# Inner weight products in plain fp32, five pairs' sums on TensorE, the identity by DMA

## Chip, core and metric

The kernel runs on one core of one Trainium2 chip. The metric is device time in microseconds (us) of one execution; the time of a kernel is the median of its runs. The engines are TensorE (PE in the rows, its weight loads PEld), VectorE (DVE), ScalarE (ACT), GpSimd (POOL) and SyncE (SP), which issues the DMAs.

## What is computed

Attention with an exponential feature map over 8 batches, 8 heads, 576 positions, then two MLPs over the positions' 512 columns:

```python
# q, k, v: (8, 8, 576, 64), w_phi: (64, 128)
def phi(x):
    proj = x @ w_phi
    proj = proj - max(abs(proj), axis=-1)
    return concat([exp(proj), exp(-proj)], axis=-1)
kv  = sum_s phi(k)[s, f] * v[s, d]
z   = sum_s phi(k)[s, f]
x   = (phi(q) @ kv) / (phi(q) @ z + 1e-6)      # heads side by side: (8, 576, 512)

gate = sigmoid(causal_conv5(x, conv_w))        # per column
y    = (gate * (x @ w_val)) @ w_out            # first MLP

h   = relu(y @ w_in)                           # 512 -> 1024: u and v halves
v_n = normalize(v over its 512 columns)
out = (u * (w_spatial @ v_n + b_spatial)) @ w_out2
```

`w_val`, `conv_w`, `w_out`, `w_in` and the second `w_out` arrive as float64. `w_out` and `w_in` stand behind each other with nothing between, so the kernel forms their product once ("inner" weights `wg` for the half `v`, `wu` for the half `u`).

## The kernel before

The program is written as a plan: every instruction is added with the engines that could do it, the buffers it reads and writes and a key (its due time), and `Plan.order` sorts them into one queue for each engine with modelled durations, allocating two SBUF arenas on the way: `fa` (fp32, `FA_COLS` columns) and `ra` (fp32r, the rest of 28,880). Changing keys, an arena's size or an instruction therefore moves instructions on all engines. Copies out of PSUM may go to ScalarE or VectorE, as the plan decides. All ScalarE and VectorE work is recorded at one helper line (L378 before, L379 after), products at L434/L447 before and L435/L448 after, GpSimd at L413/L414, DMAs at L423/L424.

The work has three parts. *Weights* (`weights`): each float64 matrix is loaded as 128x1024 words, turned into fp32 by one ScalarE and four VectorE instructions (`load_f64`: ScalarE's absolute value, then two TENSOR_SCALAR and two SCALAR_TENSOR_TENSOR), and split by `split`/`parts` into a high and a low fp32r part (a copy, a subtraction on VectorE); a product of two such pairs takes three fp32r products (high x high, low x high, high x low). The inner weights are 4 blocks of 128x512 for `wg` and 4 for `wu`, each of 4 x 3 products (`gemm`); a block is copied to its high part by ScalarE and its low part by VectorE. *Attention* (`attention`), for 32 pairs of heads (4 per batch): load k and v (`load_k`), project k (`kproj`), exponentials (`kexp`), key-value sums (`kvacc`), feature sums z (`ksum` adds four blocks on VectorE, 2 + 2 instructions of 512 and 256 columns a head; `ztotal` sums over partitions on TensorE), a transpose against the identity (`kvturn`), project q (`qproj`), the maximum over partitions by GpSimd's `partition_all_reduce`, exponentials (`qexp`), `weigh` (es0 * z0 + es1 * z1: one ScalarE and one VectorE instruction of 576 columns a head), numerator and denominator on TensorE (`num`), and the division (`divide`), whose reciprocals go through DRAM (`rden`) to be broadcast. *MLP* (`mlp`) for each of the 8 batches, with `val` first: `wv` against x.

GpSimd's queue begins with `make_identity` (a memset and a select, masks.py), then memsets of `k4` and `v4`, the tiles that hold the last 64 positions of a pair's k and v in a block pattern, then of `ones`, `mine`, `s2`, `wr2`, and only then the maxima. SyncE's queue takes DMAs in the plan's order and waits in line for each buffer.

Of the kernel before, what the change touches and what calls it, by code (L numbers as in the profile page):

```python
# [34 lines left out]
AQ_LOAD, AQ_PROJ, AQ_EXP, AQ_NUM, AQ_HEAD, A_DIV = 0.1, 0.857, 1.733, 2.5, 0.965, 4.437  # L35
W_VAL, W_CONV, W_OUT, W_G, W_U, W_SP, W_OUT2, W_STEP = -1.593, -1.22, -0.852, -0.752, -0.564, -0.207, 0.466, 0.085
M_CONV, M_VAL, M_V, M_U, M_SP, M_OUT, M_ALL = -0.153, -0.295, -0.088, -0.004, 0.003, 0.195, 57.899
LONG_W, LONG_A, LONG_M = False, True, False
WINDOW = 0.341
FA_HOLD = 1000  # L40
RA_HOLD = 5009
PA_HOLD = 0
LATER = 0.161
# [289 lines left out]
def attn_moe_gmlp_kernel(  # L333
# [132 lines left out]
    ident_t = const.tile([128, 128], F32, name="ident")  # L466
    make_identity(nc, ident_t)
# [8 lines left out]
    convw = [fixed([128, 5], F32, f"convw{c}") for c in range(KD)]  # L476
# [9 lines left out]
    def load_f64(src, n):  # L486

        raw, w = fa.buf(2 * n), fa.buf(n)
        dma(raw.bitcast(U32), src.bitcast(U32))
# [17 lines left out]
    def weights():  # L507
# [14 lines left out]
        for hh in range(2):  # L522
            for r in range(2):
                fill(mine[hh][64 * r:64 * r + 64], float(r == hh))
        for x, value in ((s2, 1.0), (wr2, 0.0)):
            fill(x.f32()[64:128], value)
        for k in range(KD):
            at(W_VAL + W_STEP * k)
            split(load_f64(rows(w_val, k), DM), wv[0][k], wv[1][k])
# [36 lines left out]
        for k in range(KD):  # L566
            at(W_OUT2 + W_STEP * k)
            split(load_f64(rows(w_out2, k), DM), wo[0][k], wo[1][k])
# [67 lines left out]
    def ztotal(kva, sums, kpl):  # L636

        mms = []
        for first in (True, False):
            for j in range(4):  # L640
                hh, s = divmod(j, 2)
                o = kva[32 * j:32 * j + 32, 2 * F:3 * F]
                mms.append((o, ones, sums[:, F * j:F * j + F], True, False) if first
                           else (o, mine[hh], kpl[:, s], False, True))
        products(2 * 4 * F / 2400 + 0.1, mms, COLS4)

    def kvturn(kva):
# [4 lines left out]
        def run():  # L652
            for s in range(3):
                nc.tensor.transpose(real(tp)[:, F * s:F * s + F], real(kvT)[:, F * s:F * s + F], ident_t)  # L654

        plan.add({"PE": (0.35, 1.0, run)}, [kvT], [tp])
# [35 lines left out]
    def num(es, kv, ts):  # L692
# [9 lines left out]
        for j in range(2):  # L702
            copy(nd[:, js[j]], accs[j][:, 0:HALF])
        acc = psum()
        products(4 * HALF / 2400 + 0.05, [
            (acc[64 * hh + 32 * j:64 * hh + 32 * j + 32, 0:HALF], ones, ts[hh][:, js[j]], True, True)
            for j in range(2) for hh in range(2)
# [19 lines left out]
    def attention():  # L727
# [5 lines left out]
        for P in range(n):  # L733
# [10 lines left out]
            sums = fa.buf(4 * F)  # L744
            for hh in range(2):
                ksum(kp[hh], sums[:, 2 * F * hh:2 * F * hh + 2 * F])
            ztotal(kva, sums, kpl)
# [6 lines left out]
            for hh in range(2):  # L754
# [3 lines left out]
                ts.append(weigh(hh, es[hh], kv))  # L758
# [7 lines left out]
    def mlp(b):  # L766
# [5 lines left out]
        for c in range(KD):  # L772
# [6 lines left out]
                "ACT": act_way(a, x[:, 0:S], ACTF.Copy, scale=convw[c][:, 0:1]),  # L779
                "DVE": dve_way("tensor_scalar", out=a, in0=x[:, 0:S], scalar1=convw[c][:, 0:1], scalar2=None,  # L780
# [201 lines left out]
```

## Time and profile before

| | us |
|---|---|
| three runs | 909.77, 913.94 (median), 914.80 |
| profiled execution | 913.05 |
| its span | 911.3 |
| TensorE busy | 860.2 (94%) |
| VectorE busy | 724.6 (80%) |
| ScalarE busy | 533.6 (59%) |
| GpSimd busy | 154.7 (17%) |

The busy shares are means over a start of some 125 us, in which weights are prepared and the first pairs run, and a long part in which attention and MLP alternate. They are to be read by stretch, not over the whole span.

### The profile page before, as it was taken

Reading aid. Unit: us, or ns where it says so; the run is one execution under the profiler, and the core shown is the slowest. Engines: PE = TensorE matmul, PEld = TensorE weight load, DVE = VectorE, ACT = ScalarE, POOL = GpSimd, SP = SyncE. Lnnn points to the kernel's source line nnn. Section 1 sums busy time; section 2 is a strip of 40 time slices with the busy share of each in tenths; the row PEclk is TensorE's granted clock in tenths of the full one; section 3 lists DMA queues with packets and bytes.
Section 4 is the critical chain, followed back from the end, with each engine's and each line's share of the span. In section 5 each row is a group of like instructions: output and inputs, shape, how many; then the busy total and the mean of one; then the engine's idle time right before and its main releaser. Section 6 shows DMA issues by size and latency. Waiting matters only on the chain.

```text
span 911.3 us, 16890 instructions
## 1 busy us (share of the span) xinstructions
PE 860.2 (94%) x6224; PEld 679.8 (75%) x6224; DVE 724.6 (80%) x1674; ACT 533.6 (59%) x1124; POOL 154.7 (17%) x121
## 2 busy tenths in 40 slices
PE   4575999999999999999999999999999999999998
PEld 2342677688777888778777888778777888789896
DVE  3989999899869997589768997598768997497551
ACT  3577757675656765466557575475557665463231
POOL 3340121132012211113012211013011211100000
PEclk9787999999999999999999999999999999999999
DMA  7355313322221121221221121221220220101001
GB/s 219 102 151 155 104 54 89 100 84 61 68 78 44 43 77 50 65 60 50 80 62 37 53 86 47 72 60 51 79 64 31 70 64 31 32 21 37 24 6 58
DMA packets 60570, 61.94 MB, mean 68 GB/s; under 512 B 23366, under 2 KB 39878, under 8 KB 60488
## 3 DMA queue, kind: packets, MB, share of 16 engines
q1 hardware_dynamic: 60488, 60.87, 22.9%
q8 instruction: 49, 0.80, 0.4%
q14 instruction: 33, 0.27, 0.1%
HBM read 50.06 MB, written 9.58 MB: 65 GB/s over the span
## 4 chain that ended last, share of the span: by engine, by line
PE 77%; DVE 14%; DMA 3%; issue 3%; ACT 2%; POOL 1%; SPq 0%; ACTq 0%; DVEq 0%; POOLq 0%
PE bank L434 54%; PE bank L447 22%; DVE fa L378 12%; ACT fa L378 2%; DMA fa<-rden 1%; DVE ra L378 1%; DMA fa<-in_w_in_dram 1%; PE bank L654 1%; DMA fa<-in_w_out_dram 1%; POOL fa L413 0%; SPq L423 0%; DVE wu L378 0%; DVE wg L378 0%; ACT wv L378 0%; DVE ws L378 0%
## 5 line engine op out<-in xcount | busy, mean ns | idle before, releaser
L378 ACT ACTIVATE fa<-fa 128x576 f32<-128x576 f32 (+4 forms) x457 | 266.3, 624 | 115.7 <-DVE fa L378 92.2
L378 ACT ACTIVATE fa<-bank 128x288 f32<-128x288 f32 (+5 forms) x395 | 166.5, 451 | 165.6 <-PE bank L434 114.4
L413 POOL PARTITION_ALL_REDUCE fa<-fa x64 | 147.1, 2326 | 480.9 <-ACT fa L378 341.0
L378 DVE TENSOR_TENSOR fa<-fa 128x576 f32<-128x576 f32 (+4 forms) x368 | 171.3, 484 | 26.3 <-DMA fa<-rden 21.0
L447 PE MATMUL bank<-fa 128*64 128x288 f32 (+1 forms) x1024 | 136.1, 410 | 10.8 <-DVE fa L378 7.9
L378 ACT ACTIVATE ra<-fa 128x256 fp32r<-128x256 f32 (+5 forms) x211 | 94.8, 468 | 76.1 <-DVE fa L378 75.5
L378 DVE TENSOR_TENSOR ra<-fa,ra 128x256 fp32r<-128x256 f32 (+4 forms) x236 | 118.3, 522 | 10.4 <-ACT ra L378 10.0
L434 PE MATMUL bank<-wg,ra 128*128 128x512 f32 (+1 forms) x480 | 120.6, 401 | 0.0
L447 PEld LDWEIGHTS bank<-fa 128*64 128x64 f32 x1024 | 71.9, 140 | 63.1 <-issue 21.1
L434 PE MATMUL bank<-ws,ra 128*128 128x256 f32 (+1 forms) x768 | 113.7, 297 | 0.3 <-ACT fa L378 0.3
L434 PEld LDWEIGHTS bank<-ra,wu 128*128 128x128 f32 x768 | 104.0, 188 | 12.6 <-issue 7.7
L434 PE MATMUL bank<-ra,wu 128*128 128x256 f32 (+1 forms) x768 | 112.7, 298 | 0.0
L434 PEld LDWEIGHTS bank<-ws,ra 128*128 128x128 f32 x768 | 103.7, 188 | 9.4 <-issue 5.8
L434 PE MATMUL bank<-ra,wv 128*128 128x256 f32 (+1 forms) x768 | 109.1, 297 | 1.0 <-DVE fa L378 0.5
L378 DVE SCALAR_TENSOR_TENSOR fa<-fa 128x576 f32<-128x576 f32 (+4 forms) x208 | 103.7, 508 | 5.3 <-ACT fa L378 4.1
L434 PEld LDWEIGHTS bank<-ra,wv 128*128 128x128 f32 x768 | 102.6, 188 | 7.0 <-issue 2.8
L378 DVE SCALAR_TENSOR_TENSOR fa<-fa,convw 128x576 f32<-128x576 f32 x128 | 106.9, 856 | 1.1 <-ACT fa L378 0.9
L434 PE MATMUL bank<-wo,ra 128*128 128x512 f32 x432 | 106.1, 398 | 0.0
L434 PEld LDWEIGHTS bank<-wg,ra 128*128 128x128 f32 (+1 forms) x480 | 82.5, 177 | 29.6 <-issue 4.1
L434 PEld LDWEIGHTS bank<-wo,ra 128*128 128x128 f32 x432 | 79.4, 188 | 20.8 <-DVE fa L378 2.3
L378 DVE TENSOR_SCALAR fa<-fa 128x9 f32<-128x9 f32 (+9 forms) x199 | 56.6, 309 | 17.9 <-DMA fa<-fa 14.9
L378 DVE TENSOR_REDUCE fa<-bank 128x4 f32<-128x512 f32 (+1 forms) x96 | 51.4, 547 | 13.2 <-PE bank L447 13.0
(62 smaller groups left out, 650.0 us busy)
## 6 DMA issues: line engine op xcount, KB each, us to landing
fa<-in_qT_dram SPq DMA_DIRECT2D x32, 288.0 KB
fa<-rden SPq DMA_DIRECT2D x64, 144.0 KB
fa<-in_v_dram SPq DMA_DIRECT2D x32, 264.0 KB
fa<-in_kT_dram SPq DMA_DIRECT2D x32, 256.0 KB
out_dram<-fa SPq DMA_DIRECT2D x32, 256.0 KB
fa<-in_w_in_dram SPq DMA_DIRECT2D x8, 512.0 KB
fa<-in_w_val_dram SPq DMA_DIRECT2D x4, 512.0 KB
fa<-in_w_outT_dram SPq DMA_DIRECT2D x4, 512.0 KB
```

The lines of the kernel that those rows point to most:

```text
L378: return lambda: getattr(engine, method)(**{k: real(v) for k, v in kw.items()})
L413: getattr(nc.gpsimd, method)(*(real(a) for a in args), **{k: real(v) for k, v in kw.items()})
L434: nc.tensor.matmul(real(acc), lhsT=real(l), rhs=real(r), start=first and i == 0, stop=last and i == n - 1)
L447: nc.tensor.matmul(real(o), lhsT=real(l), rhs=real(r), start=first, stop=last)
L654: nc.tensor.transpose(real(tp)[:, F * s:F * s + F], real(kvT)[:, F * s:F * s + F], ident_t)
```

## The change

- The identity `ident` is no longer made by GpSimd: a zeroed tile is written to DRAM (`eye`), a column of ones to its diagonal, and `ident` is loaded from it, three DMAs on SyncE.
- GpSimd runs `partition_all_reduce` once on 4 columns of a zeroed tile `warm`, ahead of everything but the first memsets.
- The converted `w_out` and `w_in` are no longer split; the inner weights are formed by 4 plain fp32 products a block instead of 12 fp32r ones.
- For the first `EARLY` = 5 pairs the feature sums skip `ksum`: `ztotal` takes all four blocks of the exponentials (16 + 4 products instead of 4 + 4), and the denominator skips `weigh`: `num` takes z as weights against both exponentials (8 products instead of 4).
- The convolution weights are loaded into one tile, so that one conversion of 20 columns takes the place of four of 5.
- The plan's keys and holds, the arena's size and which arena end is used change, and with them the order everywhere.

```diff
-FA_COLS = 16416
+FA_COLS = 16944
 A_LEAD, A_RATE = 1.485, 1.0
-AK_LOAD, AK_SPLIT, AK_PROJ, AK_STEP, AK_ACC, AK_TURN = -1.619, -0.272, 0.647, -0.759, 0.582, 2.141
+AK_LOAD, AK_SPLIT, AK_PROJ, AK_STEP, AK_ACC, AK_TURN = -1.619, 0.008, 0.087, -0.449, 0.245, 2.141
...
-LONG_W, LONG_A, LONG_M = False, True, False
+LONG_W, LONG_A, LONG_M = True, False, True
...
-RA_HOLD = 5009
+RA_HOLD = 7101
...
+EARLY = 5
...
-    ident_t = const.tile([128, 128], F32, name="ident")
-    make_identity(nc, ident_t)
+    ident = fixed([128, 128], F32, "ident")
+    eye = Buf(dr.tile([128, 128], F32, name="eye"), 128)
+    warm = fixed([128, 8], F32, "warm")
...
+        fill(warm, 0.0)
+        pool(9.0, "partition_all_reduce", warm[:, 4:8], [warm], warm[:, 4:8], warm[:, 0:4], channels=128,
+             reduce_op=bass_isa.ReduceOp.absmax)
+        at(W_EYE)
+        zero, one = fa.buf(128), fa.buf(1)
+        fill(zero, 0.0)
+        dma(eye, zero)
+        fill(one, 1.0)
+        dma(eye.rearrange("a b -> (a b)")[0:128 * 128:129].unsqueeze(1), one)
+        dma(ident, eye)
...
-        for c in range(KD):
-            at(W_CONV)
-            copy(convw[c], load_f64(rows(conv_wT, c), 5))
+        at(W_CONV)
+        copy(convw, load_f64([rows(conv_wT, c) for c in range(KD)], 5 * KD))
         wot = []
         for c in range(KD):
             at(W_OUT + W_STEP * c)
-            wot.append(parts(load_f64(rows(w_outT, c), DM), DM))
+            wot.append(load_f64([rows(w_outT, c)], DM))
...
-                win.append(parts(load_f64(rows(w_in, c)[:, DM * e:DM * e + DM], DM), DM))
+                win.append(load_f64([rows(w_in, c)[:, DM * e:DM * e + DM]], DM))
...
-                gemm(acc, [
-                    t for (oh, ol), (ih, il) in zip(wot, win)
-                    for t in ((oh[:, ds], ih), (ol[:, ds], ih), (oh[:, ds], il))
-                ])
+                products(KD * 4 * DM / 2400, [
+                    (acc, o[:, ds], i, c == 0, c == KD - 1) for c, (o, i) in enumerate(zip(wot, win))
+                ], FULL)
...
+        mms, n = [], len(terms[0])
+        for i in range(n + 1):
             for j in range(4):
...
+                mms.append((o, ones, terms[j][i], i == 0, False) if i < n
+                           else (o, mine[j // 2], kpl[:, j % 2], False, True))
...
+        if ts:
+            terms = [[(ones, t)] for t in ts]
+        else:
+            z = [kv[:, 2 * F + 32 * i:2 * F + 32 * i + 32] for i in range(4)]
+            terms = [[(z[2 * hh + s], es[hh][s]) for s in range(2)] for hh in range(2)]
...
+            if P < EARLY:
+                terms = [[kp[j // 2][:, j % 2, F * c:F * c + F] for c in range(4)] for j in range(4)]
...
+                if P >= EARLY:
+                    ts.append(weigh(hh, es[hh], kv))
```

What moves where, word for word from the two orders (names: `k_`, `v_` are the k4 and v4 tiles, `fa`/`ra` the arenas, `bank` a PSUM bank; an ISA row without names is GpSimd's preparation for the call behind it).

GpSimd at the start, before:

```order
masks.py:197 MEMSET ident 128x128
masks.py:199 ISA
masks.py:199 AFFINE_SELECT ident<-ident 128x128
L413 MEMSET k_0_81 64x64 x2
...
L413 MEMSET mine_89 64x32 x2
L413 MEMSET s_90 64x512
L413 MEMSET wr_91 64x576
L413 ISA
L413 ISA fa<-fa 128x576 x4
```

and after:

```order
L414 MEMSET k_0_79 64x64 x2
...
L414 MEMSET mine_87 64x32 x2
L414 MEMSET warm 128x8
L414 ISA
L414 ISA warm<-warm 128x4
L414 MEMSET fa 128x128
L414 MEMSET fa 128x1
L414 MEMSET s_88 64x512
L414 MEMSET wr_89 64x576
L414 ISA fa<-fa 128x576 x4
```

The select ahead of the k4 memsets is gone, and the preparation for the maxima stands ahead of the dummy and the two fills for `eye` instead of ahead of the first real maximum.

VectorE up to the last instruction that the first wg products need, before (row 132, a subtraction of a split):

```order
L378 TENSOR_SCALAR fa<-fa 128x512
L378 SCALAR_TENSOR_TENSOR fa<-fa 128x512 x2
L378 TENSOR_TENSOR ra<-fa,ra 128x512
L378 SCALAR_TENSOR_TENSOR fa<-fa 128x512
...
L378 TENSOR_SCALAR fa<-fa 128x9
L378 SCALAR_TENSOR_TENSOR fa<-fa 128x576
L378 TENSOR_TENSOR ra<-fa,ra 128x512
```

and after (row 95, a conversion):

```order
L379 TENSOR_TENSOR fa<-fa 128x576
L379 TENSOR_SCALAR fa<-fa 128x512
L379 COPY fa<-bank_70 128x288
...
L379 SCALAR_TENSOR_TENSOR fa<-fa 128x512
L379 TENSOR_TENSOR fa<-bank_68,fa 128x512
L379 SCALAR_TENSOR_TENSOR fa<-fa 128x512
```

The subtractions into `ra` and the weighings (576 columns, SCALAR_TENSOR_TENSOR) are gone from the queue, and copies from PSUM have come in.

TensorE from the first wg block on, before:

```order
L447 MATMUL bank_67<-fa 64x288 x4
L447 MATMUL bank_71<-fa 64x288 x4
L434 MATMUL bank_72<-ra 128x512 x12
L434 MATMUL bank_74<-ra 128x512 x12
...
L434 MATMUL bank_73<-ra 128x512 x12
L447 MATMUL bank_74<-fa,ones 32x288 x4
L447 MATMUL bank_67<-wphi,k_2_83 128x128
```

and after:

```order
L448 MATMUL bank_69<-fa,wphi 128x288
L448 MATMUL bank_68<-fa 128x512 x4
L448 MATMUL bank_67<-fa 128x512 x4
...
L668 MATMUL bank_68<-ident,fa 128x128 x3
L448 MATMUL bank_69<-fa,v_1_83 128x256
L448 MATMUL bank_69<-fa 64x256 x8
L448 MATMUL bank_67<-fa 64x288 x4
L448 MATMUL bank_68<-fa 64x288 x4
L448 MATMUL bank_70<-fa 32x288 x8
L448 MATMUL bank_71<-wphi,k_2_81 128x128
```

A block has 4 products instead of 12, and a transpose and a pair's numerator (64x288) that stood ahead of the wg blocks now stand behind them; the first MLP product is row 129 in both orders.

## Rows read from the trace of the kernel before

**Rows 1.** Stretches: length, busy us of PE, PEld, DVE, ACT, POOL; clock; DMA share.

```profile
0.00:10.16 10.16, 0.00 (x0) 0.00 (x0) 0.00 (x0) 2.19 (x3) 0.95 (x8) 1.00 0.61 192
10.16:93.13 82.97, 52.45 (x367) 31.51 (x367) 74.06 (x146) 52.36 (x116) 26.36 (x30) 0.82 0.49 149
93.13:125.88 32.75, 30.44 (x170) 22.07 (x168) 32.18 (x56) 22.96 (x44) 2.17 (x1) 1.00 0.28 81
125.88:911.30 785.42, 777.34 (x5693) 626.20 (x5691) 618.36 (x1474) 456.07 (x963) 125.23 (x82) 1.00 0.20 57
13.02:94.62 81.60, 51.13 (x354) 30.49 (x355) 75.01 (x148) 53.44 (x119) 24.08 (x15) 0.81 0.47 143
```

**Rows 2.** The chain that ended last, in order: start us, us, what.

```profile
82.03 5.96 DMA fa<-in_w_in_dram
```

**Rows 3.** TensorE's timeline: start us, us, what xcount, idle before and its releaser.

```profile
10.16 0.80 PE L447 MATMUL bank<-wphi,k 128*128 128x128 f32 x2 [10.16 <-POOL k L413]
...
34.45 0.80 PE L447 MATMUL bank<-wphi,k 128*128 128x128 f32 x2
...
89.47 3.73 PE L447 MATMUL bank<-fa 128*64 128x288 f32 x16 [1.16 <-ACT fa L378]
...
93.13 5.81 PE L434 MATMUL bank<-ra 128*128 128x512 f32 x24
...
125.88 1.68 PE L434 MATMUL bank<-ra,wv 128*128 128x256 f32 x12
```

**Rows 4.** GpSimd's timeline, same columns.

```profile
9.52 0.28 POOL masks.py:199 TENSOR_SCALAR_AFFINE_SELECT ident<-ident 128x128 f32<-128x128 f32 x1 [8.58 <-issue]
...
19.71 5.03 POOL L413 PARTITION_ALL_REDUCE fa<-fa  x2 [5.99 <-DMA v<-in_v_dram]
```

**Rows 5.** DMA issues on SyncE's queue, same columns.

```profile
3.68 0.60 SPq L423 DMA_DIRECT2D k<-in_kT_dram  x1
...
15.01 0.43 SPq L423 DMA_DIRECT2D fa<-in_kT_dram  x1
...
52.68 0.47 SPq L423 DMA_DIRECT2D rden<-fa  x1
55.26 1.09 SPq L423 DMA_DIRECT2D fa<-rden  x2
```

**Rows 6.** ScalarE's timeline, same columns.

```profile
8.64 0.66 ACT L378 ACTIVATE fa<-fa 128x512 f32<-128x512 f32 x1 [6.63 <-DMA fa<-in_w_val_dram]
```

**Rows 7.** VectorE's timeline, same columns.

```profile
22.48 2.54 DVE L378 TENSOR_SCALAR fa<-fa 128x512 uint32<-128x512 uint32 x2
...
93.93 0.69 DVE L378 TENSOR_TENSOR ra<-fa,ra 128x512 fp32r<-128x512 f32 x1 [0.53 <-ACT ra L378]
```

**Rows 8.** VectorE's groups, 13 to 94.62: xcount | busy us, mean ns | idle before.

```profile
L378 DVE TENSOR_TENSOR ra<-fa,ra 128x512 fp32r<-128x512 f32 x9 | 7.5, 836 | 1.7 <-ACT ra L378 1.7
L378 DVE SCALAR_TENSOR_TENSOR fa<-fa 128x576 f32<-128x576 f32 x7 | 5.7, 814 | 0.9 <-ACT fa L378 0.9
L378 DVE TENSOR_TENSOR fa<-fa 128x512 f32<-128x512 f32 x8 | 5.5, 684 | 0.8 <-PE bank L447 0.8
L378 DVE TENSOR_TENSOR fa<-fa 128x256 f32<-128x256 f32 x8 | 3.3, 418 | 0.0
L378 DVE TENSOR_SCALAR fa<-fa 128x5 f32<-128x5 f32 x4 | 2.3, 620 | 0.0
```

**Rows 9.** TensorE's timeline, a pair's products in plain fp32.

```profile
51.88 2.16 PE L447 MATMUL bank<-fa 128*64 128x288 f32 x16
53.98 0.70 PE L447 MATMUL bank<-fa,v 128*128 128x256 f32 x2
54.61 1.95 PE L447 MATMUL bank<-fa 128*64 128x256 f32 x16
56.48 1.80 PE L447 MATMUL bank<-fa,wphi 64*128 64x288 f32 x8
...
105.77 0.69 PE L447 MATMUL bank<-fa,ones 128*32 128x288 f32 x8
```

More of the change, by code (lines that the diff above doesn't have):

```diff
@@ L9 @@
 from concourse._compat import with_exitstack
-from concourse.masks import make_identity
 F32 = mybir.dt.float32
@@ L475, in attn_moe_gmlp_kernel @@
     wr1 = fixed([128, S], F32R, "wr1")
-    convw = [fixed([128, 5], F32, f"convw{c}") for c in range(KD)]
+    convw = fixed([128, 5 * KD], F32, "convw")
     rden = [Buf(dr.tile([2, S], F32, name=f"rden{i}"), S) for i in range(4)]
@@ L488, in load_f64 @@
         raw, w = fa.buf(2 * n), fa.buf(n)
-        dma(raw.bitcast(U32), src.bitcast(U32))
+        m = 2 * n // len(src)
+        for i, x in enumerate(src):
+            dma(raw.bitcast(U32)[:, m * i:m * i + m], x.bitcast(U32))
         words = raw.bitcast(U32).rearrange("p (n t) -> p n t", t=2)
@@ L528, in weights @@
             at(W_VAL + W_STEP * k)
-            split(load_f64(rows(w_val, k), DM), wv[0][k], wv[1][k])
-        for c in range(KD):
-            at(W_CONV)
-            copy(convw[c], load_f64(rows(conv_wT, c), 5))
+            split(load_f64([rows(w_val, k)], DM), wv[0][k], wv[1][k])
+        at(W_CONV)
+        copy(convw, load_f64([rows(conv_wT, c) for c in range(KD)], 5 * KD))
         wot = []
@@ L567, in weights @@
             at(W_OUT2 + W_STEP * k)
-            split(load_f64(rows(w_out2, k), DM), wo[0][k], wo[1][k])
+            split(load_f64([rows(w_out2, k)], DM), wo[0][k], wo[1][k])
     xt = {}
@@ L634, in ksum, with ztotal @@
             op=ALU.add)
-    def ztotal(kva, sums, kpl):
-        mms = []
-        for first in (True, False):
+    def ztotal(kva, terms, kpl):
+        mms, n = [], len(terms[0])
+        for i in range(n + 1):
             for j in range(4):
-                hh, s = divmod(j, 2)
                 o = kva[32 * j:32 * j + 32, 2 * F:3 * F]
-                mms.append((o, ones, sums[:, F * j:F * j + F], True, False) if first
-                           else (o, mine[hh], kpl[:, s], False, True))
-        products(2 * 4 * F / 2400 + 0.1, mms, COLS4)
+                mms.append((o, ones, terms[j][i], i == 0, False) if i < n
+                           else (o, mine[j // 2], kpl[:, j % 2], False, True))
+        products((n + 1) * 4 * F / 2400 + 0.1, mms, COLS4)
     def kvturn(kva):
@@ L653, in run @@
             for s in range(3):
-                nc.tensor.transpose(real(tp)[:, F * s:F * s + F], real(kvT)[:, F * s:F * s + F], ident_t)
-        plan.add({"PE": (0.35, 1.0, run)}, [kvT], [tp])
+                nc.tensor.transpose(real(tp)[:, F * s:F * s + F], real(kvT)[:, F * s:F * s + F], real(ident))
+        plan.add({"PE": (0.35, 1.0, run)}, [kvT, ident], [tp])
         copy(kv, tp[:, 0:3 * F])
@@ L704, in num @@
         acc = psum()
-        products(4 * HALF / 2400 + 0.05, [
-            (acc[64 * hh + 32 * j:64 * hh + 32 * j + 32, 0:HALF], ones, ts[hh][:, js[j]], True, True)
-            for j in range(2) for hh in range(2)
+        if ts:
[3 more added lines that the diff above has]
+            terms = [[(z[2 * hh + s], es[hh][s]) for s in range(2)] for hh in range(2)]
+        n = len(terms[0])
+        products(n * 4 * HALF / 2400 + 0.05, [
+            (acc[64 * hh + 32 * j:64 * hh + 32 * j + 32, 0:HALF], w, x[:, js[j]], i == 0, i == n - 1)
+            for i in range(n) for j in range(2) for hh in range(2) for w, x in (terms[hh][i],)
         ], COLS4)
@@ L743, in attention @@
             at(t, AK_TURN)
[L744 to L747, printed above, removed]
+            if P < EARLY:
+                terms = [[kp[j // 2][:, j % 2, F * c:F * c + F] for c in range(4)] for j in range(4)]
+            else:
+                sums = fa.buf(4 * F)
+                for hh in range(2):
+                    ksum(kp[hh], sums[:, 2 * F * hh:2 * F * hh + 2 * F])
+                terms = [[sums[:, F * j:F * j + F]] for j in range(4)]
+            ztotal(kva, terms, kpl)
             kv = kvturn(kva)
@@ L757, in attention @@
                 at(t, AQ_HEAD * hh + AQ_NUM)
-                ts.append(weigh(hh, es[hh], kv))
+                if P >= EARLY:
+                    ts.append(weigh(hh, es[hh], kv))
             nd, dn = num(es, kv, ts)
```

16 lines of the change are left out of this document (8 added, 8 removed).

## Prediction

> **What bounds the kernel now.** I cut the span into stretches first, then read the start in detail. The stretches [rows 1] tell where TensorE's missing 51 us of 911.3 are: 10.16 before its first product, 82.97 − 52.45 = 30.5 between 10.16 and 93.13, 2.3 between 93.13 and 125.88, and only 8.1 in the 785.42 us from the first product of the MLP (125.88) to the end. Between 10.16 and 93.13 it also works at a mean granted clock of 0.82, from 93.13 on at 1.00. So from 93.13 on TensorE is the limit, and what the change can win lies before. There VectorE sets the pace: it can only begin at 13.02, when the first projection is out, and from then to 94.62 it works for 75.01 of 81.60 us [rows 1]. The chain agrees: it runs through VectorE's conversions and one weight load (82.03, 5.96 us [rows 2]) before TensorE takes over.
>
> Three landmarks on TensorE matter [rows 3]: the first product at 10.16, released by a memset of GpSimd; the first inner weight product (wg) at 93.13; the first MLP product (wv) at 125.88. The changed order has the same six key projections, six query projections, five key-value sums, four numerators and four denominators ahead of the last landmark, so the kernels can be compared landmark by landmark.
>
> **Start of the span.** GpSimd does nothing until 9.52 (8.58 us without a releaser), then the select; the memsets of k4 behind it release TensorE at 10.16 [rows 3, 4]. The change takes the select away, so the memsets run from 0.8 on, and the first product waits for its loads: the last one of k4 is issued at 3.68 [rows 5]. The row next to it is the first w_val load, 32 times as large, issued at 4.96 and used by ScalarE at 8.64: 3.7 us [rows 5, 6]. The shortest trip here is rden's, written from 52.68 and read from 55.26: 2.6 us [rows 5]. So the k4 data is there between 6.3 and 7.4; I take 6.7. That moves TensorE, and VectorE behind it, forward by 3.5 us (2.8 to 3.9): VectorE begins at 9.5 instead of 13.02.
>
> The pause of 5.99 us before the first real maximum [rows 4] now falls before the dummy, between about 3.5 and 12. I count no gain for that beyond the 3.5: the maximum waits for projections that come 3.5 earlier. Its price: the first maxima ran 2.5 us each, and two VectorE instructions under them took 2.54 us together [rows 4, 7]. The dummy has 4 columns instead of 576, and no row shows such a size: it holds VectorE up by between 0 and 2.5 us. I take 0, since most of it falls before VectorE has much to do, and keep 2.5 for the range. The Trainium skill, GPSIMD Engine Reference, section 8 (Key points), has a rule against this part: GpSimd shares its SBUF interfaces with VectorE, with contention for VectorE instructions in a 2-port mode or with two SBUF inputs. The 2.54 us row agrees; by the rule the sum would be worse by up to the same 2.5 us.
>
> The identity's three DMAs stand on SyncE's queue between the convolution weights and pair 2's loads. Each takes SyncE 0.3 to 0.7, two wait for the one before (2.6 us as for rden), the first for a buffer that VectorE gives back. So pair 2's loads, issued from 15.01 on [rows 5], go out up to 8 us later. Pair 2's projection ran at 34.45 [rows 3]: the cover is over 10 us, and I cost it at nothing; without cover it would be those 8 us.
>
> **VectorE's work before the inner products.** Up to 94.62 it takes 147 instructions, the last being the subtraction at 93.93 that the wg products need [rows 7]. The changed order needs 103, to the last conversion of w_outT. By groups [rows 8]: nine splits of inner weights 9 × 0.836 = 7.5 us; seven weighings for denominators 7 × 0.814 = 5.7; eight and eight feature sums 8 × 0.684 + 8 × 0.418 = 8.8; of the convolution weights' sixteen small instructions, four of which took 2.3, four are left, about 3.3 less; part of one w_in load that no longer comes ahead, 3.1. Together 28.4. Back come three copies from PSUM and part of one more key exponential, 3.2. Net 25 of 86.5.
>
> Wall time per summed time was 81.60/86.5 = 0.94. If that stays, the remaining 61 take 58 us. If instead what disturbs VectorE stays whole (the ten 576-column instructions, most of them behind maxima, are ten in both orders), only undisturbed time goes: the groups sum to 86.5 where VectorE was busy 75.01, so each of 147 begins 0.08 before the one ahead ends, a 128x512 one is worth 0.60, and the same count gives 18.8 net: 62.8 us. With the start at 9.5 the last conversion is done between 67.5 and 72.3. The first inner block needs it only for its last quarter, 2.7 us after it began, so the block starts between 64.8 and 72.3. I take **70**, near the slower end because of those maxima, against 93.13: 23.1 us earlier. ScalarE (53.44 of 81.60 us busy [rows 1], with nine copies fewer) doesn't bind. Six of the eight weight loads for wg stand on SyncE's queue ahead of pair 0's rden write, the last one right behind pair 1's, at about 61 by VectorE's order, so it has some 5 us in hand.
>
> **TensorE from the first inner product to the first MLP product.** Before: 32.75 us, 30.44 busy, 23.1 of it in 96 fp32r products of 128x512 (0.24 each: 5.81 for 24 [rows 3]). After: 32 plain fp32 products of this size, which the trace lacks. Bounds from fp32 rows, start to start [rows 9]: a 128x128x256 one takes 0.63 with a change of tiling behind it (53.98 to 54.61), and 256 further columns cost 1.87/4 = 0.47 (54.61 to 56.48), so at most 1.10. Without the change of tiling two pairs of column halves give 1.87/4 for 256 and 2.10/4 for 288 columns (51.88 to 53.98), both 1.82 ns a column, so 0.93. Less is not excluded, since these run two side by side and may hinder each other: an fp32r product of 512 columns loses nothing of the kind at 0.24, so I let it go down to 0.85. I take 0.93, because four such products run back to back on one bank: 29.8 us.
>
> Also in this stretch now: pair 3's numerator (2.1), a transpose (0.5), twelve more column products for a feature sum and four for a denominator. A denominator's four took 0.69 [rows 9], so 0.7 and 3 × 128/288 × 0.69 = 0.9. Sum: 30.4 − 23.1 + 29.8 + 4.2 = 41.3 busy and 2.3 idle as before, 43.6: 10.9 more than 32.75. VectorE's instructions there sum to about 34, so TensorE sets the end. The other four feature sums and three denominators lie before 70, where TensorE was idle for 30 of 83 us: 4 × 0.9 + 3 × 0.7 = 5.7 more, nothing on the path. After the first MLP product one denominator of the five is left: 0.7.
>
> **Sum.** 911.3 − 23.1 + 10.9 + 0.7 = 899.8 of span; the profiled execution took 913.05, 1.75 more than its span, so 901.5, and as the forecast **901**. That execution lies 0.9 below the median of the three runs (913.94; 909.77 to 914.80), so 0.5%, 4.6 us, is about what can be told from no change.
>
> **Rivals.**
> (a) VectorE's disturbances shrink in proportion and TensorE finds no idle time: inner products at 64.8, the stretch 2.3 shorter: 901.5 − 5.2 − 2.3 = 894. For it: VectorE idles little even now. Against: the maxima, nine before 94.62, stay about as many.
> (b) The weights come no earlier: their loads wait in line on SyncE behind rden and k4 loads, as in the chain's 5.96 us load. If the inner products start at 82 to 87, the longer fp32 stretch eats the rest: 913.5 to 918.5. Against: DMA works at half its share there (0.49 [rows 1]), and six of the loads now stand before pair 0's rden write, where three did.
> (c) Slower: TensorE runs the fp32 block at the lower of its two clock levels (1.2 GHz). A pair's numerator took 3.73 us at 89.47 after an idle gap, 2.16 at 51.88 [rows 3, 9]. All the way at that level the 32 products cost 29.8 us more: 931. It decides from the point where half of them run low (916). Against: the stretch from 93.13 on had 1.00 in the dense work of the block itself [rows 1].
> (d) The whole program's order is new, and the last 785 us are no longer kept at 99%: one per cent more idle is 7.9 us, so 909. VectorE works 618 of 785 us there [rows 1], which speaks against more.
>
> **How the numbers follow.** Forecast 0.55, (a) 0.13, (b) 0.13, (c) 0.06, (d) 0.13. The range, 892 to 912, reaches from (a) with 0.85 per product (2.6 less) over 907 (1.10 per product, 5.4 more) and (d), with the late start of 72.3 on top, to the edge of (b). Faster by over 0.5% takes the forecast, (a) and over half of (d): 0.76. Within 0.5%: the rest of (d) and most of (b), 0.15. Slower: (c) and the far end of (b), 0.09.
>
> **What would show it.** The first product near 6.7 and VectorE's first row near 9.5; the dummy before 14; wg products from about 70 at 0.93 us each and a granted clock of 1.00; the first wv product near 113.6; the rest within 2 us of 786. If the wg start lies above 80, the loads or a new wait on VectorE are to blame and the term of 23.1 is wrong; if 32 products take over 34 us, that of 29.8; if the rest is over 790, it was wrong to take the long part as unchanged.

## The result, and the profile after

The changed kernel took **902.6 us** (median of 4 runs, 900.6 to 904.75), the kernel before 912.69 in the same series (4 runs, 909.77 to 914.80): ratio 0.9892, 95% interval 0.9853 to 0.9931. The forecast was 901 with a range of 892 to 912. The profiled execution took 900.6, the lowest of the four; its span is 898.8.

The three landmarks of the prediction cut the span. The columns are those of [rows 1]: length, busy time of TensorE, its weight loads, VectorE, ScalarE and GpSimd, granted clock, DMA share, GB/s.

```profile
7.11:71.77 64.66, 49.75 (x467) 30.52 (x467) 54.66 (x103) 38.90 (x83) 20.63 (x15) 0.92 0.61 183
71.77:110.47 38.70, 38.32 (x188) 18.49 (x186) 32.95 (x58) 23.94 (x45) 4.55 (x3) 1.00 0.36 106
110.47:898.80 788.33, 776.98 (x5701) 630.69 (x5699) 633.50 (x1496) 445.67 (x933) 128.24 (x82) 1.00 0.21 57
```

TensorE's timeline at the same places, to be laid beside [rows 3] (a plain fp32 product of 128x512 stands as two records, so x8 is a block of four products):

```profile
7.11 0.77 PE L448 MATMUL bank<-wphi,k 128*128 128x128 f32 x2 [7.11 <-DMA k<-in_kT_dram]
...
71.77 3.70 PE L448 MATMUL bank<-fa 128*128 128x512 f32 x8
75.68 7.13 PE L448 MATMUL bank<-fa 128*128 128x512 f32 x16 [0.21 <-DVE fa L379]
82.99 3.70 PE L448 MATMUL bank<-fa 128*128 128x512 f32 x8 [0.17 <-DVE wg L379]
...
95.05 14.00 PE L448 MATMUL bank<-fa 128*128 128x512 f32 x32
...
110.47 6.01 PE L435 MATMUL bank<-ra,wv 128*128 128x256 f32 x48
...
123.92 2.15 PE L448 MATMUL bank<-fa 128*32 128x288 f32 x16 [3.19 <-ACT fa L379]
```

| landmark, us | before | forecast | after |
|---|---|---|---|
| first product | 10.16 | 6.7 | 7.11 |
| first inner product | 93.13 | 70 | 71.77 |
| from there to the first wv product | 32.75 | 43.6 | 38.70 |
| from there to the end | 785.42 | 786.1 | 788.33 |
| span | 911.3 | 899.8 | 898.8 |

The inner products begin 21.4 us earlier, their stretch is 6.0 longer, the rest 2.9 longer: 911.3 − 21.4 + 6.0 + 2.9 = 898.8. The chain that ended last runs through a weight load that is issued beside the first inner block and lands behind it (75.48), then through TensorE up to the first wv product, and behind that through a load of the spatial weights, which ends in the wait of 3.19 us above.

```profile
70.54 4.94 DMA fa<-in_w_in_dram
...
87.02 22.03 PE bank L448 x140
...
111.46 9.56 DMA fa<-in_w_spT_dram
```

### The profile page after: what moved, and what is told of

Same layout as the page of the kernel before. It is cut to its first block, busy times and chain, and to the rows that moved or that the text cites. A ratio compares the mean times of both kernels' runs of the same rounds, so it can differ in the third digit from the quotient of the medians.

```text
span 898.8 us, 17083 instructions
## 1 busy us (share of the span) xinstructions
PE 865.1 (96%) x6352; PEld 679.7 (76%) x6352; DVE 721.1 (80%) x1655; ACT 509.8 (57%) x1061; POOL 156.4 (17%) x123
## 4 chain that ended last, share of the span: by engine, by line
PE 81%; DVE 8%; DMA 5%; ACT 3%; issue 2%; SPq 1%; DVEq 0%; ACTq 0%
PE bank L435 53%; PE bank L448 27%; DVE fa L379 7%; ACT fa L379 2%; PE bank L668 1%; DMA fa<-in_w_spT_dram 1%; DMA fa<-in_w_in_dram 1%; DMA fa<-rden 1%; SPq L424 1%; DVE ra L379 1%; DMA fa<-fa 0%; DMA k<-in_kT_dram 0%; DMA rden<-fa 0%; DMA v<-in_v_dram 0%; DVE wg L379 0%
## 5 line engine op out<-in xcount | busy, mean ns | idle before, releaser
L379 ACT ACTIVATE fa<-fa 128x576 f32<-128x576 f32 (+2 forms) x447 | 257.1, 624 | 123.8 <-DVE fa L379 95.1
L379 ACT ACTIVATE fa<-bank 128x288 f32<-128x288 f32 (+4 forms) x352 | 149.9, 453 | 164.0 <-PE bank L435 86.5
L379 DVE TENSOR_TENSOR fa<-fa 128x2 f32<-128x2 f32 (+4 forms) x348 | 161.8, 481 | 53.6 <-DMA fa<-rden 37.4
L448 PE MATMUL bank<-fa 128*64 128x256 f32 (+3 forms) x1168 | 168.1, 420 | 10.3 <-ACT fa L379 9.8
L448 PEld LDWEIGHTS bank<-fa 128*64 128x64 f32 (+2 forms) x1168 | 84.8, 140 | 83.4 <-issue 32.0
L379 ACT ACTIVATE ra<-fa 128x256 fp32r<-128x256 f32 (+4 forms) x198 | 86.6, 461 | 80.8 <-DVE fa L379 67.8
L379 DVE TENSOR_TENSOR ra<-fa,ra 128x256 fp32r<-128x256 f32 (+4 forms) x224 | 104.2, 490 | 15.3 <-ACT ra L379 12.8
L379 DVE SCALAR_TENSOR_TENSOR fa<-fa 128x2 f32<-128x2 f32 (+4 forms) x192 | 95.1, 499 | 11.1 <-ACT fa L379 8.4
L379 DVE SCALAR_TENSOR_TENSOR fa<-fa,convw 128x576 f32<-128x576 f32 x128 | 103.8, 828 | 0.0
L379 DVE TENSOR_SCALAR fa<-fa 128x512 f32<-128x512 f32 (+8 forms) x190 | 56.5, 321 | 11.3 <-ACT fa L379 6.3
```

What stands on the lines that cost most here:

```text
L379: return lambda: getattr(engine, method)(**{k: real(v) for k, v in kw.items()})
L448: nc.tensor.matmul(real(o), lhsT=real(l), rhs=real(r), start=first, stop=last)
```

## Experiments

A table of start keys sets the order of the whole program here, so an edit can be undone in two ways: with the order made anew by the table of the changed kernel, or with its order held. The ratio is to the kernel before in the same series (911.93 us for e1 to e9, 912.26 for h1 to h4, 912.84 for the last four). The times are medians, the landmarks and spans those of one profiled execution each; that of t1 took 900.95 and that of t2 911.66, the lowest of theirs. Where the order is made anew, the work ahead of a landmark can differ too.

| run | us | ratio to before (95%) | first product | first inner | first wv | span |
|---|---|---|---|---|---|---|
| changed kernel | 902.6 | 0.9892 (0.9853–0.9931) | 7.11 | 71.77 | 110.47 | 898.8 |
| e9, larger ring only | 917.56 | 1.0060 (1.0042–1.0078) | 7.22 | 68.48 | 125.22 | 915.8 |
| e1, EARLY = 0 | 927.27 | 1.0171 (1.0154–1.0188) | 7.38 | 79.75 | 134.39 | 924.1 |
| e2, inner weights in fp32r | 911.9 | 0.9987 (0.9969–1.0005) | 7.49 | 70.91 | 116.60 | 907.7 |
| e3, start as before | 911.92 | 1.0001 (0.9983–1.0020) | 9.83 | 72.05 | 130.10 | 911.2 |
| h1, VectorE +1 | 917.39 | 1.0053 (1.0028–1.0077) | 7.38 | 82.15 | 124.89 | 915.7 |
| h2, VectorE +3 | 946.04 | 1.0376 (1.0350–1.0402) | 7.24 | 97.53 | 146.00 | 942.8 |
| h3, dummy first | 901.28 | 0.9887 (0.9863–0.9911) | 7.33 | 71.89 | 110.32 | 898.7 |
| h4, half the inner products | 900.64 | 0.9872 (0.9855–0.9889) | 7.22 | 71.40 | 111.13 | 899.0 |
| h6, half as many again | 914.52 | 1.0023 (1.0006–1.0041) | 7.47 | 70.24 | 121.76 | 912.8 |
| h7, late start | 906.65 | 0.9931 (0.9906–0.9955) | 11.49 | 74.83 | 113.39 | 905.2 |
| t1, fp32r, own table | 904.84 | 0.9911 (0.9884–0.9938) | 8.89 | 71.58 | 113.46 | 899.0 |
| t2, EARLY = 0, own table | 913.96 | 1.0012 (0.9995–1.0029) | 7.17 | 72.58 | 120.76 | 909.6 |

### The order by itself

```diff
-FA_COLS = 16944
+FA_COLS = 17200
```

> The changed kernel with nothing but a larger ring of buffers (17200 columns of FA_COLS instead of 16944). No work is added or taken away; the planner only orders it a little differently. It is the control for the next run, which needs this ring, and it prices what a re-planned order alone does. Both theories below: landmarks within 2 us of the changed kernel's (first product 7.1, first inner product 71.8, first wv product 110.5, span 898.8), time within 3 us of it. If it lies further off, an order that only happens to be better or worse is worth as much as the edits, and differences of that size between the other runs say little.

Measured: 917.56, 15.0 us over the changed kernel, with the same instructions in another order. Both theories expected 3 at most.

```profile
7.22:68.48 61.26, 45.16 (x393) 26.66 (x393) 53.10 (x99) 37.86 (x82) 20.55 (x15) 0.92 0.58 180
68.48:125.22 56.74, 50.68 (x278) 25.13 (x278) 35.24 (x60) 29.08 (x56) 7.41 (x5) 0.94 0.28 85
125.22:915.80 790.58, 776.53 (x5683) 631.14 (x5681) 633.17 (x1495) 441.96 (x925) 123.06 (x81) 1.00 0.20 57
```

The inner products even begin 3.3 us earlier, but TensorE's busy time from the first product to the first wv product is 95.84 instead of 88.07 us (16 records more, and a clock of 0.94 in the second stretch) and its idle time 22.2 instead of 15.3; the rest is 2.3 longer. So with an order that fits less well, the edits end no better than the kernel before, and a run that undoes one edit under this table shows the edit and the misfit together. The next three have to be read so.

```diff
-FA_COLS = 16944
+FA_COLS = 17200
...
-EARLY = 5
+EARLY = 0
```

> The changed kernel with EARLY = 0: the feature sums and weighings of the first five pairs are back on VectorE, and TensorE no longer makes them (ring of 17200 columns). Theory V (VectorE's instructions ahead of the inner products set when these begin): about 24 more of them stand before the last inner weight conversion, some 11 to 14 us of VectorE; the first inner product moves from 71.8 to 81 to 86, the stretch up to the first wv product gets 1.6 us shorter because TensorE has less to do there, and the time rises by 8 to 12 us, to about the time of the kernel before. Rival R (the weights' loads, or merely the new table of start keys, set the start): the first inner product stays within 3 us of 71.8, and the time within 3 us of 901.

Measured: 927.27, 24.7 over the changed kernel, but 9.7 over the control with its ring (e9), the first inner product at 79.75, 11.3 later than there.

```diff
-FA_COLS = 16944
+FA_COLS = 16416
...
-            wot.append(load_f64([rows(w_outT, c)], DM))
+            wot.append(parts(load_f64([rows(w_outT, c)], DM), DM))
...
-                products(KD * 4 * DM / 2400, [
-                    (acc, o[:, ds], i, c == 0, c == KD - 1) for c, (o, i) in enumerate(zip(wot, win))
-                ], FULL)
+                gemm(acc, [
+                    t for (oh, ol), (ih, il) in zip(wot, win)
+                    for t in ((oh[:, ds], ih), (ol[:, ds], ih), (oh[:, ds], il))
+                ])
```

> The changed kernel with the inner weights again split in two parts and multiplied as three fp32r products (96 instead of 32). Theory V: five to eight splits of 0.6 to 0.8 us return to VectorE ahead of the first inner product and the others behind it; it begins 4 to 7 us later, at 76 to 79; TensorE's block of inner products takes 23.1 instead of 27.9 us, so that the stretch to the first wv product falls from 38.7 to about 34, unless VectorE's splits then set it; the time is within 3 us of the changed kernel's: the plain fp32 products win on VectorE what they cost on TensorE. Rival R: the start stays at 71.8, the block is 4.8 us shorter, and the time falls by 5 us, to about 896.

Measured: 911.9. The first inner product is at 70.91, neither later by 4 to 7 us nor with a gain behind it. The ring is that of the kernel before, so the order is another as well. Against a misfit of up to 15 us this prices nothing.

```diff
+    make_identity(nc, ident_t)
...
-        pool(9.0, "partition_all_reduce", warm[:, 4:8], [warm], warm[:, 4:8], warm[:, 0:4], channels=128,
-             reduce_op=bass_isa.ReduceOp.absmax)
...
-        dma(ident, eye)
```

> The changed kernel with the identity built on GpSimd again and without the dummy maximum. Theory V: the first product is at 10.2 instead of 7.1, VectorE's first row at 13.0 instead of 9.9, and all behind it is later by 3.1 us: first inner product at 75, time +3 us, about 904.5. Rival R1 (the start is not passed on, since the loads set the inner products' start): the first inner product stays at 71.8, time unchanged. Rival R2 (the dummy and the three DMAs cost as much as the early start brings): first inner product at 71 to 72 in spite of the first product at 10.2.

Measured: 911.92, three times the loss expected, with the first inner product at 72.05 and the first wv product at 130.10. The order moved again: 68 records of TensorE more stand ahead of the first wv product than in the changed kernel, and the rest is 7.2 us shorter (781.10). What this run does show is GpSimd's row: the select is back, and with it the pause of [rows 4].

```profile
9.19 0.28 POOL masks.py:199 TENSOR_SCALAR_AFFINE_SELECT ident<-ident 128x128 f32<-128x128 f32 x1 [8.25 <-issue]
```

### VectorE, with the order held

From here on the order is that of the changed kernel, word for word. The extra instruction is issued with the last one of each conversion, and the planner doesn't know of it.

```diff
+            last()
+            for _ in range(1 if n == DM else 0):
+                nc.vector.scalar_tensor_tensor(out=real(power), in0=real(w), scalar=1.0, in1=real(w),
+                                               op0=ALU.mult, op1=ALU.add)
```

> The changed kernel with its instruction order held word for word, and one extra VectorE instruction of 128x512 behind each of the twenty conversions of 512 columns (its result is not used); thirteen to fourteen of these lie ahead of or beside the first inner products. An undisturbed conversion instruction of this size lasts 0.68 us and begins 0.60 after the one ahead of it, so about 12 x 0.6 to 0.7 = 7.2 to 8.4 us are added to VectorE before the first inner block is complete. Theory V (VectorE's work sets the start of the inner products and the time follows it one for one): the first inner product moves from 71.8 to between 77 and 80, the first wv product from 110.5 to between 116 and 120, the span from 898.8 to 904 to 908. Rival R (the weights' loads or SyncE's queue set it, or VectorE's 8 us of idle time before 76 take the work up): first inner product at or below 74, span at most 901.

With three instead of one:

> As the run with one extra VectorE instruction for each conversion, but with three: some 22 to 25 us added to VectorE ahead of the first inner products, which is about what the edits took away from it, with the instruction order held. Theory V: first inner product at 91 to 97, which with the early start of 3 us is where the kernel before has it (93.1); span 919 to 925. Rival R: the first two thirds are taken up by idle time; first inner product at 80 to 86, span at most 914. A third outcome, a slope well under one for both doses, would mean that VectorE sets only part of the path there.

The extra instructions (L510) up to the first inner product, in the run with one and in the run with three: count | busy us, mean ns | idle time ahead of them.

```profile
L510 DVE SCALAR_TENSOR_TENSOR fa<-fa 128x512 f32<-128x512 f32 x11 | 8.6, 785 | 5.8 <-DMA fa<-fa 5.5
```

```profile
L510 DVE SCALAR_TENSOR_TENSOR fa<-fa 128x512 f32<-128x512 f32 x33 | 25.8, 782 | 7.3 <-DMA fa<-fa 6.3
```

The stretch up to the first inner product in the two runs, and the row on TensorE that stands at 53.38 in the changed kernel:

```profile
7.38:82.15 74.77, 52.16 (x467) 31.29 (x467) 61.55 (x114) 38.99 (x83) 21.34 (x15) 0.86 0.50 153
...
62.58 3.68 PE L448 MATMUL bank<-fa 128*64 128x256 f32 x14 [4.08 <-ACT fa L379]
```

```profile
7.24:97.53 90.29, 53.90 (x468) 31.96 (x468) 76.46 (x136) 39.05 (x83) 20.80 (x15) 0.85 0.42 130
...
72.81 3.68 PE L448 MATMUL bank<-fa 128*64 128x256 f32 x14 [7.00 <-ACT fa L379]
```

8.6 us of extra work move the first inner product by 10.4 us, 25.8 us by 25.8. Up to the first wv product they are 12.1 and 36.2 us, and it moves by 14.4 and 35.5. So VectorE has no slack: what is added to it arrives about one for one, and not only up to the first inner product, as the prediction had it, but up to the first wv product. The times rise by 14.8 and 43.4, where 5 to 9 and 20 to 26 were expected: I had counted the conversions ahead of the first inner product alone, and those behind it count too. Even behind the first wv product, where the last 12 of h2's 60 extra instructions sum to 9.3 us, the rest is 8.5 us longer than in the changed kernel. Rival R falls.

By VectorE's busy time, in which instructions overlap a little, the two doses add 6.9 and 21.8 us up to the first inner product, and its idle time there grows by 3.2 and 3.8. From one dose to the other, 14.9 us more of busy time move the first inner product by 15.4. Why the first dose brings some 3 us of idle time with it isn't settled.

The delay is there well before the inner products: the wait on TensorE that ends at 53.38 in the changed kernel ends 9.2 and 19.4 us later. These runs add work; what taking work away brings they don't show.

### TensorE in the inner products

```diff
-            for o, l, r, first, last in mms:
+            for o, l, r, first, last in mms[:emit]:
...
-                    (acc, o[:, ds], i, c == 0, c == KD - 1) for c, (o, i) in enumerate(zip(wot, win))
-                ], FULL)
+                    (acc, o[:, ds], i, c == 0, c == 1) for c, (o, i) in enumerate(zip(wot, win))
+                ], FULL, emit=2)
```

> The changed kernel with its order held, but only two of the four contraction parts of each inner weight product are computed (16 plain fp32 products of 128x512 instead of 32, so the MLP runs on wrong weights): 16 x 0.87 = 13.9 us less for TensorE between the first inner product and the first wv product. Theory V as the prediction has it (TensorE sets this stretch, VectorE is close behind: it was busy 33 of the 38.7 us): the stretch shrinks only until VectorE binds, to 33 to 36 us, so the span falls by 3 to 6 us. Rival (TensorE alone sets it): the stretch falls to 25 and the span by 13 to 14 us. Rival (it is hidden): the span stays within 1.5 us.

Measured: 900.64, nothing gained. TensorE is busy 26.70 us instead of 38.32 in a stretch that is as long as before, and now it waits for VectorE:

```profile
71.40:111.13 39.73, 26.70 (x155) 12.87 (x155) 34.20 (x59) 24.62 (x48) 4.58 (x3) 0.93 0.36 109
```

```profile
76.39 1.98 PE L448 MATMUL bank<-fa 128*128 128x512 f32 x4 [3.01 <-DVE fa L379]
...
108.07 0.90 PE L668 MATMUL bank<-ident,fa 128*128 128x128 f32 x3 [5.65 <-DVE wu L379]
```

"TensorE sets this stretch and VectorE is close behind" would have given 3 to 6 us; "hidden" is what came. VectorE's busy time of 34 us was the wrong measure of its path: with its waits the path takes the whole 39.7. The chain of this run passes between VectorE and ScalarE in this stretch, with 6.0 us of the attention's products and 3.31 us for rden's broadcast among them, and no inner product is on it. The transpose and the query projection at its end take 0.90 and 2.29 us, where they take 0.49 and 1.24 in the changed kernel (granted clock of the stretch 0.93 instead of 1.00), so some 1.5 of the 39.7 us are the price of the lower clock.

```diff
-            for o, l, r, first, last in mms:
+            for o, l, r, first, last in [(o, l, r, True, True) for o, l, r, *_ in mms[:again]] + mms:
```

> The changed kernel with its order held; the first two of the four contraction parts of every inner weight product are multiplied twice (48 plain fp32 products of 128x512 instead of 32, the result is the same): 16 x 0.87 = 13.9 us more for TensorE between the first inner product and the first wv product. The run with half of the products left out (16 fewer) did not shorten the span, and there the chain runs through VectorE. Theory B (two limits meet: TensorE's work and VectorE's end at the same time in this stretch): less of either gives nothing, more of TensorE's costs all of it: the first wv product moves from 110.5 to 123 to 125, the span to 911 to 914. Theory D (VectorE alone sets the stretch, TensorE has slack in it): the first wv product moves by less than 8 us, the span stays below 907.

```profile
70.24:121.76 51.52, 51.52 (x220) 24.75 (x219) 34.58 (x60) 24.99 (x48) 4.55 (x3) 1.00 0.25 80
```

TensorE has no idle time left, the stretch is 12.8 us longer for 16 products, and the time 11.9. The first wv product, at 121.76, is a little ahead of the 123 to 125 expected, because the inner products began 1.5 us earlier, and far outside theory D. Theory B holds: in this stretch the two engines' paths end together. Taking work from TensorE alone, or a cheaper product there, gains nothing; giving it more costs nearly all of it.

### The start

```diff
-        for op in self.order(window, hold):
+        for op in self.early + [o for o in self.order(window, hold) if o not in self.early]:
...
+        plan.early = plan.ops[-2:]
```

> The changed kernel with its order held on every engine but GpSimd, where the dummy maximum and the memset of its input stand ahead of all other memsets, so that whatever GpSimd spends on preparing its first library call lies ahead of k4's memsets, as it did with the select in the kernel before. Theory V: the first product comes at 10 to 14 instead of 7.1, VectorE's first row as much later, and the first inner product and the span are later by about the same 3 to 7 us. Rival R (the inner products' start does not hang on the start of the chain): first product late, first inner product within 1.5 us of 71.8, span within 2 us of 898.8.

Measured: 901.28, and the first product is not late. The dummy stands as 0.39 us and the memsets follow it at once:

```profile
0.96 0.39 POOL L414 PARTITION_ALL_REDUCE warm<-warm  x1
1.23 1.13 POOL L414 MEMSET k<- 64x64 f32 x6
```

So the start of 10.16 in the kernel before came from the pause ahead of the select, not from any first library call (what the select waits for, no row shows), and this run couldn't test what a late start costs. Memsets could:

```diff
+            for _ in range(18):
+                nc.gpsimd.memset(real(s2.f32()[64:128]), 1.0)
+            run()
```

> The changed kernel with its order held and 18 memsets of 64x512 on GpSimd (0.47 to 0.52 us each, on a tile that is filled again later) ahead of k4's memsets, so that the first product comes at about 10.2 as in the kernel before, instead of at 7.1; the dummy maximum and the identity's loads stay. Theory V, the prediction's term (a start that is 3.1 us later moves all of VectorE's work and so the inner products): first inner product at 74 to 75, span +2.5 to +3.5, time 904 to 907. Rival R: other waits on the way (for loads, for GpSimd's maxima) take the delay up, first inner product within 1 us of 71.8, span within 1 us of 898.8.

```profile
11.49 0.79 PE L448 MATMUL bank<-wphi,k 128*128 128x128 f32 x2 [11.49 <-POOL k L414]
...
74.83 3.70 PE L448 MATMUL bank<-fa 128*128 128x512 f32 x8
```

They took 10.34 us together, more than planned, so the first product is 4.4 us later, the first inner product 3.1, the first wv product 2.9, the time 4.1 us. About seven tenths of a late start arrive; the 3.05 us that the change won at the first product are worth some 2 us at the first wv product. The rest of the span is 3.5 longer here than in the changed kernel, though nothing in it was touched; in h3 and h4 it was within 0.5, in h6 2.7 longer. By the medians the time rises by 1.1 us more than the first wv product is late, so I take most of it for scatter between executions, which the runs don't settle.

### With tables that fit

To price two edits without the misfit, keys and ring were searched for each composition.

```diff
-EARLY = 5
+EARLY = 6
...
-            wot.append(load_f64([rows(w_outT, c)], DM))
+            wot.append(parts(load_f64([rows(w_outT, c)], DM), DM))
```

> The changed kernel with the inner weights split again and multiplied in fp32r, EARLY = 6 instead of 5, and a table of start keys and a ring that were searched for this composition (by the end that the kernel's own planner reckons, which is 8 us earlier than for the changed kernel). The run with fp32r and the table of the changed kernel took 911.9. Theory K (the plain fp32 products carry little or nothing of the gain: they free VectorE of the splits but give TensorE as much; the table that fits carries the rest): 892 to 902, no slower than the changed kernel. Theory F (the plain fp32 products are needed for the gain): 906 to 913, as with the old table.

Measured: 904.84 (900.95 to 906.76), between the two ranges expected, with an interval that overlaps that of the changed kernel. The planner's 8 us did not come; but neither are 911.9 the price of fp32r. With fp32r and a sixth pair's sums on TensorE the kernel is 2.2 us slower, within the scatter; what plain fp32 is worth with five pairs isn't shown.

```diff
-EARLY = 5
+EARLY = 0
```

> The changed kernel with EARLY = 0 (feature sums and weighings of the first five pairs on VectorE) and a table of start keys and a ring that were searched for it in the same way. With the table of the changed kernel it took 927.3. Theory V (VectorE's work ahead of the first wv product sets the time, so that no table makes up for it): 908 to 916, about as the kernel before, first wv product at 118 to 126. Theory K (the table makes up for it): 900 to 906.

Measured: 913.96, as the kernel before. The stretch from the first inner product to the first wv product, and the rest:

```profile
72.58:120.76 48.18, 42.31 (x204) 19.84 (x202) 41.14 (x70) 30.52 (x62) 12.09 (x8) 1.00 0.29 88
120.76:909.60 788.84, 775.07 (x5675) 631.43 (x5673) 625.11 (x1516) 437.33 (x909) 128.33 (x80) 0.99 0.21 58
```

VectorE is busy 41.14 us in the stretch where the changed kernel has 32.95. With a fitted table of its own this composition, with early start and plain fp32 but without the sums on TensorE, gains nothing that can be measured (that no better table exists isn't shown, and the kernel before wasn't given a new one); the first wv product is 5.1 us earlier than before, and 3.4 of these are lost behind it. No version tried beats the changed kernel beyond the scatter.

## Why the prediction was right, and where it was not

**What bounds the start.** Right in the main: VectorE has no slack up to the first wv product (h1, h2), and with its sums and weighings back on it the gain is gone (t2). The first inner product came 1.8 us later than taken, inside the 64.8 to 72.3 worked out from VectorE's instructions. The last conversion that its block needs is done at 72.07, 62.2 us after VectorE's first row: that is the 62.8 of the count in which what disturbs VectorE stays whole, not the 58 of the other.

```profile
71.39 0.68 DVE L379 SCALAR_TENSOR_TENSOR fa<-fa 128x512 uint32<-128x512 uint32 x1
```

The way in which VectorE holds up the block was only half of it. The prediction let the block begin 2.7 us before that conversion is done; it began 0.3 before, and not because it waited for it. TensorE's own queue was not through: from the end of a wait at 53.38 up to 71.77 it is busy for 18.34 of 18.39 us with the attention's products ahead of the block.

```profile
53.38 3.68 PE L448 MATMUL bank<-fa 128*64 128x256 f32 x14 [4.97 <-ACT fa L379]
56.98 1.89 PE L448 MATMUL bank<-fa,ones 128*32 128x128 f32 x32
...
69.37 1.08 PE L448 MATMUL bank<-fa,ones 128*32 128x128 f32 x32
...
70.60 1.24 PE L448 MATMUL bank<-fa,wphi 64*128 64x288 f32 x8
```

The lower clock that rival (c) feared in the inner products had its price here instead: the mean granted clock from 53.38 to 71.77 was 0.86, and the first two rows behind the wait of 4.97 us take 3.68 and 1.89 us, where 16 such records took 1.95 at 54.61 in [rows 9] and 32 of the second kind take 1.08 at 69.37. By these rows I estimate it at 2.8 us.

So VectorE's work arrives at the inner products by way of the attention's products too, and in the changed kernel TensorE has next to no idle time from 53.38 up to the first wv product; in the kernel before that began at 93.13. The rival of weights that come no earlier (b) is excluded, since the inner products start at 71.77 and not at 82 to 87; w_in's load of 4.94 us on the chain lands beside them.

**First product.** Forecast 6.7 from the trip of k4's load, measured 7.11; the trip from the issue at 3.68 took 3.4 us, and the memsets are long done. That all of it arrives at the inner products was too much: about seven tenths do (h7).

**The dummy.** Taken at 0, measured 0.39 us on GpSimd at 3.96, with VectorE's first row at 9.91: nothing to hold up. Nor did the pause of 5.99 us move ahead of it, as the prediction had it: it begins 0.1 us after the memset before it.

```profile
3.73 0.11 POOL L414 MEMSET warm<- 128x8 f32 x1
3.96 0.39 POOL L414 PARTITION_ALL_REDUCE warm<-warm  x1
...
16.05 5.08 POOL L414 PARTITION_ALL_REDUCE fa<-fa  x2
```

What it brings is small too. From the first product to the first real maximum it takes 8.94 us in the changed kernel (16.05 − 7.11) and 8.96 in h7; without it 9.55 in the kernel before and 9.58 in e3: 0.6 us. The Trainium skill, GPSIMD Engine Reference, section 2.1 (Instruction dispatch), says that the first call to a freshly loaded kernel pays a load of about 6 us that no row shows. By that the dummy would save up to 6 us; the rows here show 0.6. The pause of 5.99 of [rows 4] was for the most part a wait for the first query projection, whose products end at 16.99, and its copies out of PSUM. No run left out the dummy alone with the order held, so what it is worth stays open.

**Maxima and VectorE.** Under the first two real maxima, from 16.05 on, a subtraction of 128x512 takes 1.34 us where it takes 0.69 ahead of them:

```profile
15.19 0.69 DVE L379 TENSOR_TENSOR wv<-fa,wv 128x512 fp32r<-128x512 f32 x1
...
17.18 1.34 DVE L379 TENSOR_TENSOR wv<-fa,wv 128x512 fp32r<-128x512 f32 x1 [0.36 <-ACT wv L379]
```

The Trainium skill's rule that the prediction cited (GPSIMD Engine Reference, section 8, Key points: shared SBUF interfaces, contention for VectorE instructions with two SBUF inputs) agrees with that. The row of 2.54 us that the prediction put beside it is of two instructions with one SBUF input each, for which no row shows the rule's other condition, the 2-port mode. The rule didn't speak against the dummy, which met no VectorE instruction.

**The stretch of inner products.** Mis-sized by 4.9 us (43.6 forecast, 38.70). The term of 32 products at 0.93 = 29.8 measured 3.70 + 7.13 + 3.70 + 14.00 = 28.5, the sixteen wu products back to back 0.875 each, inside 0.85 to 1.10; the clock stayed at 1.00, so (c) did not come. The other work was 9.8 instead of 11.5, the idle time 0.4 instead of 2.3, carried over from the kernel before with no reason. "TensorE sets the end" was half of it: h6 bears it out, h4 shows VectorE's path ending at the same time. The net of the two fp32 terms was nearly nothing in my sum as well (7.5 us of splits off VectorE, 29.8 − 23.1 = 6.7 more on TensorE), and t1, with a sixth pair, doesn't speak against that.

**The rest.** Forecast 786.1, measured 788.3: 2.2 more, most of it the wait of 3.19 us behind w_spT's load. Rival (d) was the right mechanism in a small size.

**What I had wrong about the order.** I let the new table cost nothing ahead of the first wv product and put its risk into the last 785 us. e9 shows it the other way round: a table that doesn't fit costs 15 us, and it is the first wv product that comes 14.8 later, while the rest is 2.3 longer. The forecast held because the table that came with the change fits, which the prediction had no way to tell: 917.56 would have lain outside its range. That is luck, and so is in part the nearness of the sum: the errors of the terms, +1.8, −4.9 and +2.2, cancel in part, and the span came out 1.0 below the forecast.

**Which part carries the gain.** The feature sums and denominators on TensorE (t2: 11.4 us more without them, with a table of its own; e1 against e9, both with an ill-fitting one: 9.7). The start brings some 2 us (worked out from h7). For plain fp32 no gain clear of the scatter is shown (t1, with a sixth pair). These don't split the 10.1 us into parts: t2 alone loses all of them.

## What to carry over

Where an order is made by a table, first run the same work in another order: the size of that difference is the least that an undone edit has to show, and the other edits are better tested with the order held. In a stretch where two engines end together, moving work from one to the other pays only until they meet; busy time doesn't show where that is, since the waits on an engine's path belong to it, and halving one side's work does. Work that is added to an engine shows only that it has no slack; what less work brings has to be tried by taking some away.

## What the runs showed of the hardware

A plain fp32 product of 128x512 takes 0.875 us back to back, against 0.24 for one of fp32r ([rows 3]), so it is dearer than three fp32r products (0.72) by a fifth; I had expected 0.93. A partition maximum over 4 columns stands as 0.39 us on GpSimd where one over 576 columns takes 2.1 to 2.5, and the next memset follows it at once even where it is GpSimd's first such call (h3). A pause of 8.25 to 8.58 us stands ahead of the select in both kernels that have one.
